# Two-layer network behind bucketed attention: one list-scheduled order for all instructions, a changed row statistic, VectorE low parts, and PV in three parts

## The chip, the cores and the metric

One core of one Trainium2 chip runs the whole program. The metric is the device time of one execution in microseconds (us); lower is better.

## The reference, cut to what matters

`q`, `k`, `v` have the shape (2, 8, 768, 64): 2 batches, 8 heads, 768 rows, 64 columns. Each row of `q` and `k` gets a 6-bit bucket from the signs of its product with `proj`; a row attends only to rows of its own bucket.

```
mask = q_bucket[:, :, :, None] == k_bucket[:, :, None, :]
scores = np.where(mask, scale * (q @ k^T), -1e9)
attn = exp(scores - max); attn = attn / (sum(attn) + 1e-9)
x = (attn @ v) as 1536 tokens x 512
h = x @ w_in                      # layer 0, 512 -> 2048
P = a0 + a1*h + a2*h^2 + a3*h^3;  Q = 1 + |b0|*|h| + |b1|*h^2
x = (P / (Q + 1e-6)) @ w_out      # 2048 -> 512
h = x @ w_in2                     # layer 1
out = (h * clip(h + 3, 0, 6) / 6) @ w_out2
```

## The kernel before, in words

Every fp32 matrix is split into a high part that TensorE takes as it is and a low part (what is left of the value), and a product is made of high x high, high x low and low x high.

**Attention** works on 48 groups (`NG`): a group is 256 query rows of one head, 3 groups to a head, 16 heads in 8 pairs. For a group, `s_mm` makes two score tiles of 128 x 768 on TensorE (two PSUM buffers), `s_max` takes the negated row maximum on VectorE (line 363), `s_exp` makes the exponentials and their row sum on ScalarE into `p`. The row statistics follow: `norm_a` adds 1e-9 and takes the reciprocal on VectorE (lines 375, 376), `norm_v` flags empty rows on GpSimd (line 381), `norm_b` blends the two on VectorE (the helper at line 48, tile `stat`). `norm_p` scales `p` on GpSimd (line 391). `p_mm` transposes `p` on TensorE in three pieces `tt` (line 400), `p_hi` copies each to a high part `pth` on ScalarE (the helper `act`, line 45), `p_lo` subtracts to a low part `ptl` on VectorE (line 413), and `v_mm` multiplies both by `v` in 12 matmuls (line 421). `v_cp` and `v_add` (line 439) join the halves of the result, and `x_hi`, `x_lo` (lines 451, 459) write the two parts of `x`.

For each coming pair of heads, `load_qk` loads q and k, `tp_mm` transposes them (line 227), `tp_hi` writes the high part `th` and a full copy `tf` on ScalarE, `tp_lo` subtracts on GpSimd (line 242), `spread` lays the parts out in `q1`, `q2`, `k1`, `k2` by six DMAs inside SBUF (line 250), `z_mm` and `z_bits` make the bucket bits, and `spread_bits` lays those out (line 272). All DMAs are issued by the SyncE queue (SP).

The order is written out by hand: `slot` goes through the list `SLOT` of 33 operations for s = 0 to 47, each with a lag in groups (scores 0 or one ahead, transposes 2, PV 3, x 4), and each engine takes its instructions in that order.

**Weights** come as 32 units per layer (`order`). A unit is loaded as a 64-bit float block `raw` (line 90), turned into fp32 by `conv_a` and `conv_r` (ScalarE), `conv_s` (VectorE, line 107) and `conv_add` (GpSimd, line 111), and split by `conv_hi` and `conv_lo` (lines 119, 126). The first 11 units (`NPRE`) are converted inside the attention slots; their loads wait, by `pace`, for a score matmul. The next 8 have their place only when the pool `ate` is released, and the last 13 when `atl` is released.

**Layers** run as 96 steps (2 layers x 3 token blocks x 16 column tiles). A step is 12 matmuls into `h` (line 523), a chain on ScalarE and VectorE (helpers at lines 45 and 48), `e_hi` and `e_lo` (line 581), and 12 matmuls into `acc` (line 592). Their order comes from a list scheduler: `plan` gives each operation its engines with durations, a rank and its dependencies, and `ordered` plays them in model time. The last four slots of attention (those for s = 48 to 51) and this list are merged by time with the factor `JOIN`.

## Time and profile before

| | us |
|---|---|
| median of 3 runs | 845.35 |
| lowest, highest | 842.57, 847.24 |
| the profiled execution: device time | 845.65 |
| the profiled execution: span from first to last instruction | 843.9 |
| TensorE busy in the span | 791.7 |
| VectorE busy | 598.9 |
| ScalarE busy | 546.7 |
| GpSimd busy | 405.4 |

The device time of the profiled execution is 1.75 us above its span. Matmuls are pipelined and their ends are modelled, so TensorE's busy time holds overlaps and is not time at its peak; where it matters, starts of consecutive matmuls are compared. Durations of GpSimd are rough. An instruction's own duration can hold time in which it was held up after its start.

### The profile page before, as it was taken

The page shows a single profiled execution, that of the slowest core. Times are in us where ns is not written, and L with a number is a line of the kernel's source. Part 1 is how long each engine was busy: PE and PEld are TensorE (multiplying, and loading weights), DVE is VectorE, ACT ScalarE, POOL GpSimd, SP SyncE. Part 2 cuts the span into 40 slices and gives each one's busy share as a digit, 9 for nine tenths or more (in the row PEclk, how much of TensorE's full clock was granted, in tenths as well). Part 3 has the DMA queues.
Part 4 walks back from the last instruction along what each step waited for, and adds up shares of the span by engine and source line. Part 5 has one row for each costly group of instructions (what it writes and reads, how often), then busy time and mean ns, then how long its engine had stood idle before and what let it go on. Part 6 is the DMA issues. An engine that isn't in the chain of part 4 may idle for free.

```text
span 843.9 us, 12016 instructions
## 1 busy us (share of the span) xinstructions
PE 791.7 (94%) x4042; PEld 665.4 (79%) x4042; DVE 598.9 (71%) x995; ACT 546.7 (65%) x1014; POOL 405.4 (48%) x421
## 2 busy tenths in 40 slices
PE   7998989899888969979999999999999999999997
PEld 5887878888777748757888888888888878887885
DVE  5898989789899788988887798987862232222222
ACT  5988888798889679876768678766671222222221
POOL 5898788788888457762214276657440000000000
PEclk8999999999999979999999999999999999999999
DMA  7754446444552033440002021223420000001001
GB/s 184 188 140 122 115 118 156 105 113 113 135 140 75 11 108 126 146 135 0 1 1 75 1 76 51 75 75 119 154 103 1 13 37 1 1 0 51 1 1 50
DMA packets 46765, 65.72 MB, mean 78 GB/s; under 512 B 28808, under 2 KB 30856, under 8 KB 46704
## 3 DMA queue, kind: packets, MB, share of 16 engines
q1 hardware_dynamic: 46704, 64.96, 27.5%
q8 instruction: 32, 0.52, 0.3%
q14 instruction: 29, 0.24, 0.1%
HBM read 43.00 MB, written 3.15 MB: 55 GB/s over the span
## 4 chain that ended last, share of the span: by engine, by line
PE 64%; DVE 17%; ACT 7%; DMA 6%; issue 4%; POOL 1%; SPq 1%; DVEq 0%; ACTq 0%; POOLq 0%
PE h L523 29%; PE acc L592 27%; PE o L421 4%; DVE ptl L413 4%; DVE stat L363 3%; DVE t L48 3%; DMA q<-th 3%; PE tt L400 2%; DVE stat L375 1%; ACT p L45 1%; DVE bt L266 1%; ACT pth L45 1%; DVE xt L439 1%; DMA nqk<-in_k_dram 1%; ACT tf L45 1%
## 5 line engine op out<-in xcount | busy, mean ns | idle before, releaser
L581 DVE TENSOR_TENSOR gl<-t,gh 128x512 fp32r<-128x512 f32 x48 | 35.0, 728 | 136.7 <-ACT gh L45 114.1
L45 ACT ACTIVATE t<-h,cbias 128x512 f32<-128x512 f32 x48 | 33.0, 688 | 131.5 <-PE h L523 131.5
L111 POOL TENSOR_TENSOR cvd<-cvd,raw 128x512 int32<-128x512 int32 x64 | 89.0, 1396 | 51.3 <-DVE cvd L107 14.5
L581 POOL TENSOR_TENSOR gl<-t,gh 128x512 fp32r<-128x512 f32 x48 | 64.4, 1342 | 101.1 <-ACT gh L45 86.5
L391 POOL TENSOR_SCALAR p<-p,stat 128x768 f32<-128x768 f32 x96 | 93.8, 987 | 35.4 <-DVE stat L48 33.0
L413 DVE TENSOR_TENSOR ptl<-tt,pth 128x512 fp32r<-128x512 f32 x144 | 94.5, 683 | 22.1 <-ACT pth L45 21.3
L45 ACT ACTIVATE p<-s,stat 128x768 f32<-128x768 f32 x96 | 87.2, 908 | 18.2 <-DVE stat L363 17.8
L363 DVE TENSOR_REDUCE stat<-s 128x1 f32<-128x768 f32 x96 | 91.0, 949 | 1.5 <-PE s L356 1.2
L421 PE MATMUL o<-pth,sv 128*128 128x256 f32 x288 | 75.4, 298 | 17.4 <-ACT tf L45 10.1
L400 PE MATMUL tt<-ident,p 128*128 128x128 f32 x576 | 85.8, 278 | 5.7 <-POOL p L391 2.2
L45 ACT ACTIVATE pth<-tt 128x512 fp32r<-128x512 f32 x144 | 81.0, 601 | 13.5 <-PE tt L400 6.3
L45 ACT ACTIVATE gh<-t 128x512 fp32r<-128x512 f32 x96 | 60.1, 626 | 39.7 <-PE acc L592 39.6
L48 DVE SCALAR_TENSOR_TENSOR t<-t,coef,h 128x512 f32<-128x512 f32 x96 | 71.1, 744 | 17.7 <-ACT r L45 9.0
L400 PEld LDWEIGHTS tt<-ident,p 128*128 128x128 f32 x576 | 67.9, 141 | 18.2 <-ACT tf L45 4.9
L421 PEld LDWEIGHTS o<-pth,sv 128*128 128x128 f32 x288 | 54.5, 189 | 24.2 <-DVE xt L439 12.2
L421 PE MATMUL o<-ptl,sv 128*128 128x256 f32 x288 | 71.0, 283 | 0.5 <-DVE ptl L413 0.5
L48 DVE SCALAR_TENSOR_TENSOR t<-t,r 128x512 f32<-128x512 f32 x96 | 65.1, 682 | 8.6 <-ACT r L45 7.6
L592 PE MATMUL acc<-gh,wo_0h 128*128 128x512 f32 x192 | 54.9, 392 | 5.3 <-ACT gh L45 5.3
L353 PE MATMUL s<-k,q 128*128 128x384 f32 x192 | 57.6, 382 | 1.4 <-ACT p L45 1.4
L592 PE MATMUL acc<-wo_0h,gh 128*128 128x512 f32 x192 | 55.1, 393 | 0.4 <-DVE o L605 0.4
L421 PEld LDWEIGHTS o<-ptl,sv 128*128 128x128 f32 x288 | 54.8, 190 | 0.7 <-DVE ptl L413 0.7
L592 PE MATMUL acc<-gl,wo_0h 128*128 128x512 f32 x192 | 55.3, 395 | 0.0
(128 smaller groups left out, 2051.0 us busy)
## 6 DMA issues: line engine op xcount, KB each, us to landing
raw<-in_moe_w_in_dram SPq DMA_DIRECT2D x32, 512.0 KB
raw<-in_moe_w_out_dram SPq DMA_DIRECT2D x32, 512.0 KB
q<-th SPq DMA_DIRECT2D x30, 192.0 KB
k<-th SPq DMA_DIRECT2D x30, 192.0 KB
nqk<-in_q_dram SPq DMA_DIRECT2D x16, 192.0 KB
nqk<-in_k_dram SPq DMA_DIRECT2D x16, 192.0 KB
nv<-in_v_dram SPq DMA_DIRECT2D x16, 192.0 KB
out_dram<-o SPq DMA_DIRECT2D x12, 256.0 KB
```

The lines of the kernel that those rows point to most:

```text
L45: nc.scalar.activation(out=out, in_=in_, func=func, **kw)
L48: nc.vector.scalar_tensor_tensor(out=out, in0=in0, scalar=scalar, in1=in1, op0=op0, op1=op1)
L111: nc.gpsimd.tensor_tensor(out=d.bitcast(I32), in0=d.bitcast(I32), in1=raw[:, :, 0], op=ALU.add)
L353: nc.tensor.matmul(out=ps[:, n, 0:384], lhsT=q1[:, rs], rhs=k1[:, n * 384:(n + 1) * 384], start=True, stop=False)
L363: nc.vector.tensor_reduce(out=stat[g][:, rr, 0:1], in_=sps[(g, rr)][:, :, 0:384], axis=AX.XY, op=ALU.max, negate=True)
L391: nc.gpsimd.tensor_scalar(out=pt, in0=pt, scalar1=st[:, rr, 3:4], scalar2=st[:, rr, 4:5], op0=ALU.mult, op1=ALU.add)
L400: nc.tensor.transpose(ps[:, kt, rr], ptile[(g, rr)][:, c:c + 128], ident)
L413: nc.vector.tensor_tensor(out=pl, in0=live.pop(("p", g, i)), in1=f(ph), op=ALU.subtract)
L421: nc.tensor.matmul(out=o, lhsT=vs[:, kt].rearrange("p a d -> p (a d)"), rhs=pp[:, kt % 2], start=(kt == 0 and n == 0), stop=(kt == R - 1 a ...
L523: nc.tensor.matmul(out=ps, lhsT=w[:, ws], rhs=x[:, cols(m)], start=(n == 0), stop=(n == 3 * KD - 1))
L581: (nc.gpsimd if eng == "POOL" else nc.vector).tensor_tensor(out=e["gl"], in0=e["2"], in1=f(e["gh"]), op=ALU.subtract)
L592: nc.tensor.matmul(out=acc["o"][i], lhsT=lhsT, rhs=rhs, start=(t == 0 and n == 0), stop=(t == NF - 1 and n == 2))
```

## The change

All of attention is described to the list scheduler, pair by pair and group by group, beside the layers, and one order is played for the whole program after the set-up `start`. The hand-written `SLOT`, the merge with `JOIN` and the pacing of weight loads go. Planned durations, lags and the sizes of four buffer rings (PSUM banks `T`, score tiles `S`, `p`, `pt`) are constants. The two operations that make `babs` and the negated `coef` come ahead of `start`.

The row statistics: GpSimd writes two flags instead of one; VectorE adds the row sum, a constant 1e-9 and the first flag by one `tensor_reduce` over three elements, and takes the reciprocal; the blend `norm_b` goes. The low parts of q and k are made from PSUM by VectorE, and the copy `tf` and GpSimd's subtraction go. `v_hi` and `x_hi` are `tensor_scalar` with one input instead of `tensor_tensor` with a tile of zeros. `v_mm` is issued in three parts of 4 matmuls, each behind its own low part. `in_mm` is issued in four parts of 3 matmuls, each with its own dependencies. In the layers, `conv_hi` is planned for ScalarE or GpSimd only.

```diff
+W = {"S": 0.70, "M": 0.87, "E": 1.0, "NV": 0.46, "A": 0.28, "N": 0.965, "P": 0.44, "H": 0.48, "L": 0.60, "V": 0.475, "OC": 0.34,
+     "VA": 0.34, "XH": 0.35, "XL": 0.69, "TP": 0.33, "TH": 0.47, "TL": 0.50, "Z": 1.05, "ZB": 0.59, "VH": 0.50, "VL": 0.97,
+     "ca": 0.555, "cr": 0.56, "sh": 0.335, "add": 1.26, "hi": 0.52, "hi_P": 0.60, "lo": 0.60, "lo_P": 1.26,
+     "abs": 0.58, "sq": 0.49, "lin": 0.57, "lin_D": 0.66, "den": 0.66, "num": 0.66, "ln": 0.615, "ex": 0.52, "nw": 0.60, "rt": 0.66,
+     "g": 0.60, "rl": 0.57, "min": 0.60, "gh": 0.52, "f0": 0.49, "f1": 0.60, "mm": 0.2265, "dma": 0.60}
+W_LAG = {"PE": 0.25, "DVE": 0.13, "ACT": 0.16, "POOL": 0.09, "SP": 2.2, "NONE": 0.0}
+W_SLOT = 4.9
+W_SOON = 5.0
+W_OUT = 0.0
+W_PREP = 0.0
 AHEAD = 4
-W_SLOT, W_TAIL, JOIN = 6.0, 24.0, 2.4
+RINGS = {"T": 4, "S": 2, "p": 6, "pt": 4}
...
-        nc.gpsimd.tensor_tensor(out=s[:, :, hd % 2], in0=nat[("v", hd)], in1=zero, op=ALU.add)
+        nc.gpsimd.tensor_scalar(out=s[:, :, hd % 2], in0=nat[("v", hd)], scalar1=1.0, scalar2=0.0, op0=ALU.mult, op1=ALU.add)
...
-        ps = live["tp"].pop(0)
         if n == 0:
             hl[hd] = tuple(ate.tile([128, S], F32R, name=f"t{x}", tag=f"t{x}{hd % 2}") for x in "hl")
-        full = ate.tile([128, 384], F32, name="tf", tag="tf", bufs=2)
-        act(hl[hd][0][:, n * 384:(n + 1) * 384], ps, scale=qsc)
-        act(full, ps, scale=qsc)
-        live.setdefault("tf", []).append((hd, n, full))
-
-    def tp_lo():
-        for hd, n, full in live.pop("tf", []):
-            th, tl = (t[:, n * 384:(n + 1) * 384] for t in hl[hd])
-            nc.gpsimd.tensor_tensor(out=tl, in0=full, in1=f(th), op=ALU.subtract)
+        act(hl[hd][0][:, n * 384:(n + 1) * 384], live[("tp", hd, n)], scale=qsc)
+
+    def tp_lo(hd, n):
+        th, tl = (t[:, n * 384:(n + 1) * 384] for t in hl[hd])
+        stt(tl, live.pop(("tp", hd, n)), qsc, f(th), ALU.mult, ALU.subtract)
...
+
+    stats = [cpool.tile([128, 2, 7], F32, name=f"stat{i}") for i in range(4)]
+    for t in stats:
+        nc.vector.memset(t[:, :, 2:3], 1e-9)
...
+    def norm_v(g):
+        st = stats[g % 4]
+        for i, x in ((3, 2.0 ** 126), (5, 1.0 / S)):
+            nc.gpsimd.tensor_scalar(out=st[:, :, i], in0=st[:, :, 0], scalar1=BIG / 2, scalar2=x, op0=ALU.is_ge, op1=ALU.mult)
+
     def norm_a(g):
-        nm, sm, ri, av, bv = (stat[g][:, :, i] for i in range(5))
-        nc.vector.tensor_scalar(out=sm, in0=sm, scalar1=1e-9, scalar2=None, op0=ALU.add)
-        nc.vector.reciprocal(out=ri, in_=sm)
-
-    @group
-    def norm_b(g):
-        st = stat[g]
-        stt(st[:, :, 3], st[:, :, 0], BIG / 2, st[:, :, 2], ALU.is_lt, ALU.mult)
-
-    @group
+        st = stats[g % 4]
+        nc.vector.tensor_reduce(out=st[:, :, 6:7], in_=st[:, :, 1:4], axis=AX.X, op=ALU.add)
+        nc.vector.reciprocal(out=st[:, :, 4], in_=st[:, :, 6])
...
-    def v_mm(g):
+    def v_mm(g, i):
         vs = spl[g // 3]
-        o = live[("o", g)] = psum.tile([128, 256], F32, name="o", tag="T", bufs=4)
-        for kt in range(R):
-            for n, pp in enumerate(pts[(g, kt // 2)]):
-                nc.tensor.matmul(out=o, lhsT=vs[:, kt].rearrange("p a d -> p (a d)"), rhs=pp[:, kt % 2],
+        if i == 0:
+            live[("o", g)] = psum.tile([128, 256], F32, name="o", tag="T", bufs=4)
+        for kt in (2 * i, 2 * i + 1):
+            for n, pp in enumerate(pts[(g, i)]):
+                nc.tensor.matmul(out=live[("o", g)], lhsT=vs[:, kt].rearrange("p a d -> p (a d)"), rhs=pp[:, kt % 2],
                                  start=(kt == 0 and n == 0), stop=(kt == R - 1 and n == 1))
+        pts.pop((g, i))
...
+    def plan_attention():
...
+                    old = [("Z", pr - 1, 0), ("Z", pr - 1, 1), ("SPR", hd - 2)]
+                    add(("TP", hd, n), ("PE", W["TP"]), r, [("LQ", hd)] + old, lambda e, hd=hd, n=n: tp_mm(hd, n), takes=("T",),
+                        earliest=3.0 if pr == 1 else 0.0)
+                    add(("TH", hd, n), ("ACT", W["TH"]), r + 0.6, [("TP", hd, n)], lambda e, hd=hd, n=n: tp_hi(hd, n))
+                    add(("TL", hd, n), ("DVE", W["TL"]), r + 1.2, [("TH", hd, n)], lambda e, hd=hd, n=n: tp_lo(hd, n),
+                        frees=(("TP", hd, n),))
...
+            for hd in (2 * pr, 2 * pr + 1):
+                r = (g0 - 4 + 3 * (hd % 2)) * T
+                add(("SPR", hd), ("SP", 6 * W["dma"]), r, [("TL", hd, 0), ("TL", hd, 1), ("S", 3 * (hd - 2) + 2, 1)], lambda e, hd=hd: spread(hd))
+                add(("SB", hd), ("SP", 2 * W["dma"]), r + 0.1, [("ZB", pr, 0), ("ZB", pr, 1), ("SPR", hd)], lambda e, hd=hd: spread_bits(hd))
...
+        def group(g):
+            hd = g // 3
+            b = g * T
+            odd, last = hd % 2, g >= NG - 5
+            for rr in range(2):
+                add(("S", g, rr), ("PE", W["S"]), b - W_SOON + 1.9 * rr, [("SB", hd), ("SPR", hd)], lambda e, rr=rr: s_mm(g, rr), takes=("S",),
+                    earliest=4.0 if hd == 1 else 0.0)
+                add(("M", g, rr), ("DVE", W["M"]), b - W_SOON + 0.9 + 1.9 * rr, [("S", g, rr), ("N", g - 4, 1)], lambda e, rr=rr: s_max(g, rr))
+                add(("E", g, rr), ("ACT", W["E"]), b - W_SOON + 1.9 + 1.9 * rr, [("M", g, rr)], lambda e, rr=rr: s_exp(g, rr), takes=("p",),
+                    frees=(("S", g, rr),))
+            add(("NV", g), ("POOL", W["NV"]), b - W_SOON + 3.8, [("M", g, 0), ("M", g, 1)], lambda e: norm_v(g), pool)
+            add(("A", g), ("DVE", W["A"]), b - W_SOON + 5.0, [("E", g, 0), ("E", g, 1), ("NV", g)], lambda e: norm_a(g))
+            for rr in range(2):
+                add(("N", g, rr), ("POOL", W["N"]), b - W_SOON + 5.4 + rr, [("A", g)], lambda e, rr=rr: norm_p(g, rr), pool)
+            for i in range(3):
...
+            for i in range(3):
+                add(("V", g, i), ("PE", W["V"]), b + 9.3 + 0.5 * i, [("L", g, i), ("VL", hd), ("V", g, i - 1)], lambda e, i=i: v_mm(g, i),
+                    takes=("T",) if i == 0 else (), frees=(("H", g, i),))
...
+        add(("rel", "S"), ("NONE", 0.0), 0.0, [n for n in every if n[0] == "E"], lambda e: release_s())
+        add(("rel", "e"), ("NONE", 0.0), 0.0, [n for n in every if n[0] in ("S", "VL")], lambda e: release_e())
+        add(("rel", "l"), ("NONE", 0.0), 0.0, every, lambda e: release_l())
...
+        ate.release()
+        mps["mp"] = tc.alloc_tile_pool(name="mp", bufs=1, reuse_waits="tile")
+        wpool[1] = tc.alloc_tile_pool(name="wpool1", bufs=1, reuse_waits="tile")
+
+    def release_l():
+        atl.release()
+        wpool[2] = tc.alloc_tile_pool(name="wpool2", bufs=1, side="right", reuse_waits="tile")
+        acc["o"] = [psum.tile([128, TB], F32, name="acc", tag="T", bufs=4) for _ in range(4)]
...
+        convs = [(0, u) for u in order] + [(1, u) for u in order]
+        rel = {0: [], 1: [("rel", "e")], 2: [("rel", "l")]}
+        gone = [("rel", "S"), ("rel", "e")]
...
+            add(("ld", j), ("SP", W["dma"]), rank - 2 * T, [("add", j - RING["raw"])] + early, lambda e: conv_load(*key))
...
+            add(("hi", j), {"ACT": W["hi"], "POOL": W["hi_P"]}, rank, [("add", j)] + used + rel[wplace[u]], lambda e: conv_hi(*key, e),
+                port=("POOL",))
+            add(("lo", j), {"POOL": W["lo_P"], "DVE": W["lo"]}, rank, [("hi", j)], lambda e: conv_lo(*key, e), port=("POOL", "DVE"))
...
-        start()
-        for i in range(4):
-            (v_hi, v_lo)[i % 2](i // 2)
-        s_mm(0, 0)
-        for s in range(NG):
-            slot(s)
         act(babs, coef[:, 4:6], ACTF.Abs)
         nc.vector.tensor_scalar(out=coef[:, 0:4], in0=coef[:, 0:4], scalar1=-1.0, scalar2=None, op0=ALU.mult)
...
+        start()
+        for _, n, e in todo:
+            work[n][3](e)
```

## Rows read from the trace of the kernel before

**Rows 1.** Busy time by stage: us, busy (xinstructions) of each engine, TensorE clock, DMA.

```profile
16.00:279.00 263.00, 237.56 (x1632) 215.87 (x1632) 238.33 (x442) 225.13 (x461) 218.72 (x264) 0.98 0.51 126
279.00:400.00 121.00, 105.26 (x458) 84.37 (x457) 102.69 (x161) 94.87 (x172) 66.35 (x55) 0.94 0.28 92
400.00:640.00 240.00, 240.00 (x1054) 197.43 (x1053) 195.69 (x282) 172.72 (x297) 113.26 (x92) 1.00 0.20 64
```

**Rows 2.** Chain that ended last, merged: start us, us, what.

```profile
76.64 3.74 DMA q<-th
...
279.01 2.77 PE h L523 x12
...
302.97 1.30 POOL cvd L111
304.29 2.90 DMA raw<-in_moe_w_in_dram
...
821.09 16.35 PE acc L592 x70
```

**Rows 3.** Groups of instructions, whole span: busy us, mean ns; idle before, releasers.

```profile
L375 DVE TENSOR_SCALAR stat<-stat 128x2 f32<-128x2 f32 x48 | 24.3, 505 | 2.6 <-ACT p L45 2.1
L48 DVE SCALAR_TENSOR_TENSOR stat<-stat 128x2 f32<-128x2 f32 x48 | 14.6, 304 | 0.7
L242 POOL TENSOR_TENSOR tl<-tf,th 128x384 fp32r<-128x384 f32 x28 | 28.3, 1014 | 2.8 <-ACT tf L45 2.0 <-ACT pth L45 0.7
L45 ACT ACTIVATE tf<-tp,qsc 128x384 f32<-128x384 f32 x28 | 16.1, 574 | 0.0
L48 DVE SCALAR_TENSOR_TENSOR tl<-tp,qsc,th 128x384 fp32r<-128x384 f32 x4 | 2.3, 613 | 1.2 <-ACT th L45 1.2
```

**Rows 4.** Instructions on the tile `stat`: duration ns min/median/max, first and last start.

```profile
L375 DVE TENSOR_SCALAR stat<-stat x48: 161/537/902, 17.5 to 280.0; 128x2 f32<-128x2 f32 x48
L376 DVE RECIPROCAL stat<-stat x48: 167/168/170, 18.1 to 280.2; 128x2 f32<-128x2 f32 x48
```

**Rows 5.** Waits from 16 to 279 us, VectorE then ScalarE: us, times, longest us.

```profile
DVE ptl L413 <- ACT pth L45: 17.8, 10, 3.6
...
ACT th L45 <- DMA q<-th: 8.3, 5, 2.8
ACT pth L45 <- PE tt L400: 4.5, 15, 0.7
```

**Rows 6.** TensorE in order of time, a PV group: start us, us, instruction.

```profile
81.60 0.39 PE L421 MATMUL o<-pth,sv 128*128 128x256 f32 x1 [1.31 <-ACT tf L45]
81.82 0.28 PE L421 MATMUL o<-ptl,sv 128*128 128x256 f32 x1
81.94 0.28 PE L421 MATMUL o<-pth,sv 128*128 128x256 f32 x1
```

**Rows 7.** TensorE in order of time, the first steps of layer 0.

```profile
299.15 0.79 PE L523 MATMUL h<-xh,wi_0h 128*128 128x512 f32 x1 [2.85 <-DVE t L48]
299.75 0.63 PE L523 MATMUL h<-xl,wi_0h 128*128 128x512 f32 x1
300.17 0.63 PE L523 MATMUL h<-xh,wi_0l 128*128 128x512 f32 x1
...
310.83 0.79 PE L523 MATMUL h<-xh,wi_1h 128*128 128x512 f32 x1 [3.67 <-DVE t L48]
```

**Rows 8.** All engines in order of time, the set-up.

```profile
2.85 0.60 SPq L165 DMA_DIRECT2D pj<-in_proj_dram  x1
...
5.42 0.21 ACT L45 ACTIVATE pjh<-pj 128x6 fp32r<-128x6 f32 x1 [3.40 <-DMA pj<-in_proj_dram]
...
5.50 0.43 SPq L172 DMA_DIRECT2D coef<-in_moe_b_dram  x1
...
5.99 1.05 ACT L45 ACTIVATE th<-tp,qsc 128x384 fp32r<-128x384 f32 x2 [0.36 <-PE tp L227]
...
8.12 1.05 ACT L45 ACTIVATE th<-tp,qsc 128x384 fp32r<-128x384 f32 x2 [1.08 <-PE tp L227]
```

More of the change, by code (lines that the diff above doesn't have):

```diff
@@ L259, in z_mm @@
         for i, (w, t) in enumerate(ops):
[L260 to L261 removed]
+            nc.tensor.matmul(out=z, lhsT=w, rhs=t[:, n * 384:(n + 1) * 384], start=(i == 0), stop=(i == len(ops) - 1))
     def z_bits(pr, n):
@@ L638, in add_conv @@
-            used = [("u1" if u[0] == "o" else "i", free[u])] if layer else []
-            add(("hi", j), {"ACT": 0.62, "DVE": 0.96, "POOL": 0.7}, rank, [("add", j)] + used, lambda e: conv_hi(*key, e), port=("DVE", "POOL"), earliest=tail)
-            add(("lo", j), {"POOL": 1.3, "DVE": 0.69}, rank, [("hi", j)], lambda e: conv_lo(*key, e), port=("POOL", "DVE"))
-        for j in range(len(order) - NPRE):
+            used = [("u1" if u[0] == "o" else "i", free[u]) + (() if u[0] == "o" else (KD - 1,))] if layer else []
@@ L725, in ordered, with room @@
         free, port, held, out, now = {}, 0.0, None, [], 0.0
+        ends, took = {}, {r: [] for r in RINGS}
+        def room(n):
+            for r in work[n][6]:
+                if len(took[r]) >= RINGS[r]:
+                    by = freeing[took[r][-RINGS[r]]]
+                    if done.get(by, 1e9) > now + 1e-9:
+                        return False
+            return True
+        done = {}
         while len(out) < len(work):
@@ L756, in ordered @@
                 heapq.heappush(ready, item)
-            times = [v for v in free.values() if v > now + 1e-9] + [port] * (port > now + 1e-9) + [c[0] for c in coming[:1] if c[0] > now + 1e-9]
-            if not times:
+            while times and times[0] <= now + 1e-9:
+                heapq.heappop(times)
+            nxt = [v for v in free.values() if v > now + 1e-9] + [port] * (port > now + 1e-9) + times[:1]
+            nxt += [c[0] for c in coming[:1]]
+            if not nxt:
                 break
-            now = min(times)
@@ L761, in ordered @@
-        assert len(out) == len(work), [n for n in work if left[n]][:9]
-        return out
-    ends = {}
+            now = max(now, min(nxt))
+        assert len(out) == len(work), [n for n in work if n not in done][:9]
+        return out
+    psb, times = [], []
+    plan_attention()
+    plan_layers()
     todo = ordered()
     with tc.manual_schedule():
-        start()
-        for i in range(4):
-            (v_hi, v_lo)[i % 2](i // 2)
-        s_mm(0, 0)
-        for s in range(NG):
-            slot(s)
```

386 lines of the change are left out of this document (164 added, 222 removed).

## The prediction

> **What bounds the kernel now.** I read the busy time by stage first. From 400 us on, TensorE never pauses: 1054 matmuls in 240 us, one each 0.2277 us [rows 1]. Nothing in the change makes these matmuls fewer, so time can only come from before that. In the attention stage, 16 to 279 us, no engine is full, and two are close: VectorE is busy 238.3 of 263 us and TensorE 237.6, so they idle 24.7 and 25.4 us [rows 1]. ScalarE has 225.1 and GpSimd 218.7.
>
> Then the waits. Of VectorE's idle time, 17.8 us in 10 waits are for `pth`, the high part that ScalarE makes [rows 5]. The chain that ended last says why ScalarE was late: it passes through the DMA `q<-th`, once in most pairs (3.74 us in the row, five waits in all) [rows 2, 5]. `tp_hi` of the next pair overwrites the tile that `spread` is still reading; ScalarE stands behind that DMA, the copies behind it are late, and VectorE stops. The hand-written list puts both in the same slot.
>
> Last the join. Layer 0 starts at 279.0 us and TensorE's last run ends at 821.1 + 16.35 = 837.4 us [rows 2]. The 2304 matmuls of the layers at 0.2277 us are 524.6 us. About 7 us of attention's own matmuls still come after 279 us (an estimate: two to three groups' transposes and PV at about 2.7 us a group). 837.4 - 279.0 - 524.6 - 7 = 26.8 us are lost, all in the stage 279 to 400 or at block ends. The places to see: TensorE stops for 2.85 us before 299.15 and 3.67 us before 310.83, and after each stop its matmuls start 0.42 us apart, at the lower of its two clock levels [rows 7]. In the second stop the chain holds a weight's integer add on GpSimd (1.30 us) and then a weight load (2.90 us): the load could not start until a `raw` buffer was free [rows 2].
>
> **The change part by part.** The sum is made against the profiled execution, 845.65 us, which is 0.3 us above the median of 845.35.
>
> *Row statistics.* Gone from VectorE: 48 additions of 0.505 us and 48 blends of 0.304 us, 24.3 + 14.6 = 38.9 us [rows 3]. New: 48 reductions of 128x2x3. The trace has none so small. Below, 0.161 us, the shortest of the additions; above, 0.505 us, their mean [rows 3, 4]. I take 0.168 us, the reciprocal: same tile, same place in the order, and in 48 cases it stays between 167 and 170 ns, while the addition one instruction earlier spreads from 161 to 902 ns [rows 4]. The additions are thus held up by something that the reciprocal doesn't meet. New cost 48 x 0.168 = 8.1 us; net -30.8 us, at the upper bound 24.2 - 38.9 = -14.7 us.
>
> [...]
>
> *Low parts of q and k.* VectorE gains 28 operations `tl<-tp,qsc,th`; the four that the set-up already has take 0.613 us: +17.2 us. ScalarE loses 28 copies (16.1 us) and GpSimd 28 subtractions (28.3 us) [rows 3]; both have room [rows 1], so I count nothing for them. VectorE's work in attention: -30.8 + 17.2 = -13.6 us.
>
> *What is late next.* VectorE then holds 238.3 - 13.6 = 224.7 us, and TensorE with 237.6 us is the fuller engine. So the attention stage can't lose more than TensorE's 25.4 idle us, whatever VectorE gains.
>
> *PV in three parts.* The matmuls are the same, but a part that starts alone pays: after a wait, the second matmul starts 0.22 us after the first, later ones 0.12 us apart [rows 6]. 96 more starts x 0.10 = 9.6 us at most, nothing if the parts run back to back. The part's wait is for `ptl`; queued behind it on TensorE are the next groups' scores and transposes, and on these wait `s_max` and `p_hi`. More of that below.
>
> *The order.* `tp_hi` now depends in the plan on the spread that it used to collide with, and the plan gives a DMA 2.2 us after its issue; so I take that stall (up to 17.8 us of VectorE's idle time) as mostly gone. I put TensorE's idle time in this stage, with the PV starts in it, at 10 us of the 25.4, because two engines above 90% and a chain through four engines leave no schedule without gaps. Attention: 237.6 + 10 = 247.6 against 263 us, **-15.4 us**; bounds -25.4 us, and above zero if the PV waits bite.
>
> *DMAs.* The first 11 weight loads are no longer paced and stand in SP's order among `spread`, `load_qk` and `load_v`. The number of transfers is the same. A load of 2.90 us [rows 2] ahead of a spread delays it by about that; the plan ranks a spread about three slots (15 us) ahead of its scores, which covers it. Without that cover, 11 x 2.9 = 32 us would be the end.
>
> *The join.* Weight units 11 to 13 can now be loaded and taken as far as `cvd` during attention; only `conv_hi` waits for the pool. That removes the load and add that stand in the chain at 303 us. The two stops are 2.85 + 3.67 = 6.5 us, and some 20 matmuls at the lower clock cost 20 x 0.2 = 4 us. I take **-10 us**, between nothing (the remaining 18 units still have to pass through ScalarE and GpSimd beside the first steps) and -26.8 us.
>
> *Set-up.* `babs` and the negated `coef` now stand ahead of the first `th` on ScalarE and VectorE, and wait for the DMA of `coef`. It is issued until 5.93 us; the `pj` DMA, issued until 3.45, was there at 5.42, so `coef` is there at about 7.9 us. `th` started at 5.99, so the first moves by 2.1 us, the second (8.12) by about 1 [rows 8]. I take **+1.5 us** between these.
>
> `v_hi` and `x_hi` only relieve GpSimd, and its 48 further flags lie in its idle time (263 - 218.7 = 44.3 us [rows 1]): nothing. Without that cover they would come between the row sums and VectorE's reduction. Sum: 845.65 - 15.4 - 10 + 1.5 = **822 us**.
>
> **The rivals.**
>
> *Slower: TensorE waits for each PV part.* Where: in attention, on TensorE's queue, 48 x 3 = 144 waits for `ptl`, each behind two engines (`tt` to `pth` to `ptl`). At w us each, attention is 237.6 + 10 + 144w; the whole gain of 23.9 us is gone at w = 0.17 us. At 0.3 us it is 43.2 us, and the time 822 + 43 = 865 us. For it: the chain of three hand-overs is short of slack, and ScalarE already waits for TensorE's transposes 15 times for 4.5 us [rows 5]. Against: the scheduler fills TensorE with other groups' work between part and low part, and two score tiles let it run ahead. [...]
>
> *Only VectorE's work counts.* The order has as many gaps as the old one and the join is as before: 845.65 - 13.6 + 1.5 = 834 us. For it: hand-made and planned order meet the same four nearly full engines.
>
> *Packed.* Attention idles 3 us on TensorE and the join loses only 7: 845.65 - 22.4 - 20 + 1.5 = 805 us. For it: the plan knows the buffer rings and the DMA delay.
>
> *It doesn't do what it says.* The reduction is held up as the addition was, VectorE has -14.7 + 17.2 = +2.5 us, and half of the join's gain remains: 845.65 + 2.5 + 1.5 - 5 = 845 us.
>
> **How the numbers follow.** A measurement of this kernel can tell about 0.5% (4.2 us) from no change. Forecast 0.45, packed 0.16, only VectorE's work 0.16: all three faster, 0.77. Not doing what it says: 0.09, within 0.5%. TensorE waiting: 0.14, slower. The range goes from 799 (a little under the packed case) to 847 us (above the case of no effect); it leaves out the slower rival and the far side of the packed one. The forecast's own range is 812 to 832 us.
>
> **What would show it.** Right: VectorE's reduction over `stat` steady near 0.17 us; its waits for `pth` well under 17.8 us and no `q<-th` under ScalarE's; the first matmul into `h` near 265 us; no stop of several us for a weight load in layer 0's first six steps; the first `th` near 8 us. Wrong: TensorE's waits for `ptl` adding up to tens of us, the first `h` at 279 or later, or the time from the first `h` to the end of the span longer than now (843.9 - 279.0 = 564.9 us); and ScalarE waiting for `raw` loads or `spread`, which would mean that the plan's DMA delay is too short.

## The result, and the profile after

The changed kernel takes 855.78 us (median of 4 runs, 855.33 to 856.37), the kernel before on the same chip 845.53 (842.57 to 847.24): ratio 1.0125, 95% interval [1.0096, 1.0155]. It is slower by 1.25%, and the forecast of 822 us, with its range from 799 to 847 us, had the wrong sign. The profiled execution has a span of 854.6 us.

Busy time by stage, attention first, then three windows counted from the first `h` (269.7 us), columns as in [rows 1]:

```profile
16.00:270.00 254.00, 235.59 (x1667) 221.18 (x1668) 234.05 (x438) 217.36 (x449) 190.85 (x286) 0.99 0.55 137
...
269.70:390.70 121.00, 110.91 (x471) 88.42 (x470) 107.48 (x164) 91.10 (x160) 66.84 (x53) 0.95 0.25 79
390.70:630.70 240.00, 220.04 (x923) 174.25 (x922) 192.92 (x276) 149.97 (x256) 106.89 (x84) 0.98 0.20 62
```

The same two windows of the kernel before, counted from its first `h` at 278.9 us:

```profile
278.90:399.90 121.00, 105.26 (x457) 84.41 (x457) 102.69 (x161) 94.97 (x172) 66.35 (x55) 0.94 0.28 92
399.90:639.90 240.00, 240.00 (x1054) 197.40 (x1053) 195.78 (x282) 172.72 (x297) 113.36 (x92) 1.00 0.20 64
```

Two things happened. Attention became shorter: the first `h` comes 9.2 us earlier (278.9 to 269.7). The layers became longer: from the first `h` to the end, 584.9 us instead of 565.0. The join is not where it went: in the first 121 us TensorE does 14 matmuls more than before. The loss lies in the next 240 us, where [rows 1] had no pause at all: 923 matmuls instead of 1054, and 131 x 0.2277 = 29.8 us. Some of that is won back in the other windows; from the first `h` to the end the loss is 584.9 - 565.0 = 19.9 us.

The parts that the prediction costed, as groups of the whole span (with those of [rows 3], the copies `tf` and GpSimd's `tl` are gone) and on the tile `stat` (duration ns min/median/max, as [rows 4]):

```profile
L53 DVE SCALAR_TENSOR_TENSOR tl<-tp,qsc,th 128x384 fp32r<-128x384 f32 x32 | 19.0, 609 | 6.8 <-ACT th L50 6.7
```

```profile
L336 DVE TENSOR_REDUCE stat<-stat x48: 140/149/163, 20.1 to 268.4; 128x2 f32<-128x6 f32 x48
L337 DVE RECIPROCAL stat<-stat x48: 167/168/171, 20.3 to 268.6; 128x2 f32<-128x2 f32 x48
```

Waits from 16 to 270 us (us in total, times, longest), for [rows 5]:

```profile
PE s L313 <- ACT p L50: 10.5, 11, 1.9
PEld o L368 <- DVE ptl L360: 10.1, 19, 2.2
...
PE o L368 <- DVE ptl L360: 5.3, 10, 1.9
...
DVE ptl L360 <- ACT pth L50: 4.5, 11, 1.3
...
ACT th L50 <- DMA q<-th: 1.4, 1, 1.4
```

VectorE's wait for `pth` fell from 17.8 to 4.5 us, ScalarE's for `q<-th` from 8.3 to 1.4, as forecast. TensorE's idle time in the stage fell less than forecast, from 25.4 to 18.4 us (254.00 - 235.59) and not to 10: its largest wait is now for the exponentials `p`, which must have read a score tile before its buffer is used again, 10.5 us in 11. In the kernel before, from 16 to 279 us:

```profile
PE s L353 <- ACT p L45: 1.4, 4, 0.6
```

And the waits from 380 to 610 us, in layer 0, which [rows 1] had left no room for:

```profile
ACT t L50 <- DVE t L432: 40.2, 24, 2.7
ACT t L50 <- DVE t L53: 24.0, 25, 1.5
...
PE acc L492 <- ACT gh L50: 18.8, 16, 3.6
```

TensorE now waits 18.8 us for `gh`, the high part of the activation. The chain behind it shows in one step of ScalarE, VectorE and TensorE in order of time (start us, us, instruction):

```profile
427.81 0.74 DVE L432 TENSOR_SCALAR t<-h,coef 128x512 f32<-128x512 f32 x1
...
428.59 0.60 ACT L50 ACTIVATE t<-h 128x512 f32<-128x512 f32 x1 [2.22 <-DVE t L432]
...
429.09 0.62 ACT L50 ACTIVATE gh<-t 128x512 fp32r<-128x512 f32 x1
...
429.23 0.75 DVE L53 SCALAR_TENSOR_TENSOR t<-t,coef,h 128x512 f32<-128x512 f32 x1 [0.67 <-ACT t L50]
...
429.76 1.20 PE L492 MATMUL acc<-gh,wo_0h 128*128 128x512 f32 x4 [0.55 <-ACT gh L50]
...
429.89 0.74 DVE L53 SCALAR_TENSOR_TENSOR t<-t,babs,r 128x512 f32<-128x512 f32 x1
...
430.72 0.72 ACT L50 ACTIVATE t<-t,cbias 128x512 f32<-128x512 f32 x1 [1.02 <-DVE t L53]
...
431.48 0.60 ACT L50 ACTIVATE r<-t 128x512 f32<-128x512 f32 x1
...
432.12 0.69 DVE L53 SCALAR_TENSOR_TENSOR t<-t,r 128x512 f32<-128x512 f32 x1 [0.83 <-ACT r L50]
...
432.72 0.75 DVE L53 SCALAR_TENSOR_TENSOR r<-t,coef,r 128x512 f32<-128x512 f32 x1
...
433.50 0.69 DVE L53 SCALAR_TENSOR_TENSOR t<-t,r 128x512 f32<-128x512 f32 x1
...
434.11 0.74 DVE L432 TENSOR_SCALAR t<-h,coef 128x512 f32<-128x512 f32 x1
...
434.89 0.60 ACT L50 ACTIVATE t<-h 128x512 f32<-128x512 f32 x1 [2.23 <-DVE t L432]
```

Read it as a ring. VectorE's `t<-h,coef` (`e_lin`) ends; 0.04 us later ScalarE's square `t<-h` (`e_sq`) starts, after 2.22 us of idling; when that ends, VectorE's next read of `h` starts, after 0.67 us; then denominator, logarithm (1.02 us of waiting), exponential, VectorE again (0.83 us), three of its operations, and only then the next step's `e_lin`. In a round ScalarE stands for 2.22 + 1.02 us and VectorE for 0.67 + 0.83 us until the other engine has ended an operation. A round takes 434.11 - 427.81 = 6.30 us, and TensorE needs 24 x 0.2277 = 5.46 us for a step.

`e_sq` takes nothing from `e_lin`; both only read `h`. That they take turns is no dependency of the plan: for `e_sq` it lists the in-matmuls and an older `e_den`. In the rows above the square starts 0.04 us after the other read of `h` has ended (427.81 + 0.74 and 428.59, 434.11 + 0.74 and 434.89); what makes it wait is not shown. Where the list puts `e_sq` ahead of `e_lin`, it doesn't wait (433.23 in the rows of e10, below).

The same rows show a second thing that the plan doesn't have. Two operations that follow on one engine keep the planned distance where the second doesn't use the result of the first: the denominator starts 0.66 us after VectorE's read of `h` (429.23, 429.89), and 0.66 is planned. Where the second does use it, the distance is longer than planned: the exponential starts 0.76 us after the logarithm (430.72, 431.48; planned 0.615), and `e_g` 0.78 us after `e_rt` (432.72, 433.50; planned 0.66). In the 27 and 28 such pairs from 380 to 560 us that no wait parts, the medians are the same 0.76 and 0.78.

A third thing differs. `e_lin` may stand on ScalarE or VectorE, and the planner chooses by the durations. All of its instructions, the kernel before first (duration ns min/median/max, first and last start):

```profile
L45 ACT ACTIVATE t<-h,coef x33: 665/682/711, 298.0 to 558.4; 128x512 f32<-128x512 f32 x33
L532 DVE TENSOR_SCALAR t<-h,coef x15: 739/750/752, 286.0 to 553.1; 128x512 f32<-128x512 f32 x15
```

```profile
L432 DVE TENSOR_SCALAR t<-h,coef x43: 737/744/753, 274.2 to 579.4; 128x512 f32<-128x512 f32 x43
L50 ACT ACTIVATE t<-h,coef x5: 689/691/693, 282.0 to 501.0; 128x512 f32<-128x512 f32 x5
```

Before, 33 of 48 were on ScalarE, and from 380 to 610 us the square waits for `e_lin` on VectorE once, 0.3 us; now 5 are, and it waits 24 times, 40.2 us.

### The profile page after: what moved, and what is told of

It is laid out like the page before. It is cut to its first block, busy times and chain, and to the rows that moved or that the text cites. A ratio compares the mean times of both kernels' runs of the same rounds, so it can differ in the third digit from the quotient of the medians.

```text
span 854.6 us, 11830 instructions
## 1 busy us (share of the span) xinstructions
PE 796.7 (93%) x4042; PEld 670.7 (78%) x4042; DVE 607.7 (71%) x1005; ACT 522.7 (61%) x962; POOL 377.0 (44%) x439
## 4 chain that ended last, share of the span: by engine, by line
PE 45%; DVE 28%; ACT 12%; DMA 5%; issue 5%; POOL 4%; SPq 1%; ACTq 0%; POOLq 0%; DVEq 0%
PE acc L492 18%; PE h L424 17%; DVE t L53 10%; DVE ptl L360 4%; ACT t L50 4%; PE o L368 4%; DVE stat L320 3%; PE tt L349 3%; DVE t L432 2%; ACT r L50 2%; DVE r L53 2%; DVE cvd L112 2%; PE s L313 2%; DMA raw<-in_moe_w_in_dram 2%; ACT p L50 1%
## 5 line engine op out<-in xcount | busy, mean ns | idle before, releaser
L341 POOL TENSOR_SCALAR p<-p,stat 128x768 f32<-128x768 f32 x96 | 95.9, 1007 | 35.1 <-DVE stat L337 21.1
L53 DVE SCALAR_TENSOR_TENSOR t<-t,h 128x512 f32<-128x512 f32 x48 | 33.0, 687 | 101.3 <-ACT t L50 101.2
L368 PE MATMUL o<-pth,sv 128*128 128x256 f32 x288 | 81.0, 305 | 3.8 <-DVE ptl L360 3.2
L349 PE MATMUL tt<-ident,p 128*128 128x128 f32 x576 | 80.3, 274 | 1.2 <-DVE xt L385 0.7
L492 PE MATMUL acc<-gh,wo_0h 128*128 128x512 f32 x192 | 60.1, 421 | 22.6 <-ACT gh L50 21.4
L368 PE MATMUL o<-ptl,sv 128*128 128x256 f32 x288 | 77.7, 296 | 2.9 <-DVE ptl L360 2.6
L53 DVE SCALAR_TENSOR_TENSOR t<-t,r 128x512 f32<-128x512 f32 x96 | 65.7, 685 | 20.4 <-ACT r L50 18.8
L481 DVE TENSOR_TENSOR gl<-t,gh 128x512 fp32r<-128x512 f32 x47 | 37.2, 791 | 49.6 <-PE acc L492 44.9
L492 PEld LDWEIGHTS acc<-gh,wo_0h 128*128 128x128 f32 x192 | 36.3, 197 | 38.4 <-ACT gh L50 31.8
L313 PE MATMUL s<-k,q 128*128 128x384 f32 x192 | 54.8, 367 | 10.6 <-ACT p L50 10.5
```

What stands on the lines that cost most here:

```text
L53: nc.vector.scalar_tensor_tensor(out=out, in0=in0, scalar=scalar, in1=in1, op0=op0, op1=op1)
L313: nc.tensor.matmul(out=ps[:, n, 0:384], lhsT=q1[:, rs], rhs=k1[:, n * 384:(n + 1) * 384], start=True, stop=False)
L341: nc.gpsimd.tensor_scalar(out=pt, in0=pt, scalar1=st[:, rr, 4:5], scalar2=st[:, rr, 5:6], op0=ALU.mult, op1=ALU.add)
L349: nc.tensor.transpose(ps[:, kt, rr], ptile[(g, rr)][:, c:c + 128], ident)
L368: nc.tensor.matmul(out=live[("o", g)], lhsT=vs[:, kt].rearrange("p a d -> p (a d)"), rhs=pp[:, kt % 2], start=(kt == 0 and n == 0), stop=( ...
L481: (nc.gpsimd if eng == "POOL" else nc.vector).tensor_tensor(out=e["gl"], in0=e["2"], in1=f(e["gh"]), op=ALU.subtract)
```

## The experiments

Each is the changed kernel or the kernel before with the edit shown or described; `...` marks what is cut from an edit. None leaves out work.

**Where the loss is.** The first theory was that the output matmuls of a step are listed too early, three steps behind its in-matmuls. e1 lists them two steps later; e2 forces a distance of three on the kernel before; e3 puts the four in-parts back into one item.

```diff
-            ro = r + 2.5 * T
+            ro = r + 4.5 * T
```

> The changed kernel, with the planned rank of the second matmuls of a step (out_mm) two step lengths later, so that the planned order puts 5 steps' first matmuls ahead of a step's second matmuls in place of 3. Theory (no reserve): TensorE's queue in layer 0 waits for the high part gh because only three steps are in flight; with five the 21 us of these waits go, the time from the first matmul into h to the end of the span falls from 584.7 us to 565 or less, and the time is near 833 us. Rival (the split of in_mm into four parts, or the planned engines of the weight conversion, make the loss): the time stays between 850 and 858 us.

Measured 837.12 us, ratio 0.9872 [0.9835, 0.9909]; first `h` at 269.5, from there to the end 564.3. Later output matmuls take the loss away, though the square still waits 21.1 us for `e_lin` from 380 to 610 us.

```diff
-            add(("i", m), ("PE", W_MM), r, [(x, m - 2) for x in last] + wi + [("i", m - 1)], lambda e, m=m: in_mm(m))
+            add(("i", m), ("PE", W_MM), r, [(x, m - 2) for x in last] + wi + [("i", m - 1), ("o", m - 3)], lambda e, m=m: in_mm(m))
```

> The kernel before, with one more dependency in its plan: a step's first matmuls come behind the second matmuls of the step three earlier, so that 3 steps are in flight in place of 4 to 7. Nothing else is changed. Theory (no reserve): TensorE begins to wait for gh in layer 0, some 20 us are lost and the time is near 865 us. Rival: the lead doesn't matter, the time stays at 845 us within 4 us.

Measured 851.86, ratio 1.0057 [1.0035, 1.0078]. A distance of three costs the old plan some 5 us, not 20.

```diff
...
-                add(("i", m, kk), ("PE", 3 * W["mm"]), r + kk * 3 * W["mm"],
...
+            add(("i", m, KD - 1), ("PE", 12 * W["mm"]), r,
+                [(x, m - 2) for x in last] + [("i", m - 1, KD - 1)] + gone + every_i,
+                lambda e, m=m: [in_mm(m, kk) for kk in range(KD)])
```

> The changed kernel, with in_mm planned as one operation of 12 matmuls as before. The planned lead is 5 steps at the start of layer 0 but 3 from the fifth step on. Theory (no reserve): TensorE still waits for gh in layer 0, the time is 848 to 858 us. Rival (the split makes the loss): near 835 us.

Measured 859.91, ratio 1.0139 [1.0099, 1.0179], with TensorE's waits for `gh` at 21.4 us in the whole span, as in the changed kernel: the split is not the cause.

e5 leaves out the 0.15 us that the kernel before plans between dependent operations of one engine. Its planned distance falls to three, as in the changed kernel.

```diff
-                    ends[x] = max(ends.get(x, 0.0), now + c + W_LAG.get(e, W_SEM))
+                    ends[x] = max(ends.get(x, 0.0), now + c + (0.0 if work[x][0].keys() == {e} else W_LAG.get(e, W_SEM)))
```

> The kernel before, whose list scheduler lets an operation that follows one on its own engine start without the planned 0.15 us between them, as the changed kernel's does. The planned lead of TensorE falls from 4 to 7 steps to 3 or 4; the attention slots are the same. Theory (the gap made the lead): TensorE waits for gh in layer 0 as in the changed kernel, 10 to 20 us are lost, 855 to 865 us. Rival (other durations or the joined order make the loss): 845 us within 4 us.

Measured 837.41, ratio 0.9918 [0.9885, 0.995]: faster, with a distance of three, which neither expectation had. The first theory falls: the distance alone is not it.

**The planned durations.** What was left is the table `W`. The change plans the layers' operations with the spacing of operations that run back to back (den 0.66), the kernel before with their whole duration (0.74). e9 and e10 give the changed kernel the older values, e13 and e14 one half of them each, e15 gives e5 the change's.

```diff
+W.update({'abs': 0.68, 'sq': 0.58, 'lin': 0.69, 'lin_D': 0.74, 'den': 0.74, 'num': 0.74, 'ln': 0.72, 'ex': 0.6, 'nw': 0.69, 'rt': 0.74, 'g': 0.69, 'rl': 0.69, 'min': 0.69, 'gh': 0.62, 'f0': 0.59, 'f1': 0.68})
+W.update({'ca': 0.66, 'cr': 0.67, 'hi': 0.62, 'hi_P': 0.7, 'lo': 0.69, 'lo_P': 1.3, 'sh': 0.42, 'add': 1.3})
```

The first line alone is e13, the second e14, both e10; e9 also has `'mm': 0.21583`.

> The changed kernel, planned with the layer durations of the kernel before (elementwise operations 0.58 to 0.74 us where the change plans 0.49 to 0.66; conversions 0.62 to 1.30; a step of 24 matmuls 5.18 us where the change plans 5.44). The planned lead of in_mm over out_mm stays at three steps, as in the changed kernel; the work is the same, and only the order differs. Theory A (the change's short durations give an order in layer 0 in which ScalarE and VectorE take turns with nothing to spare): the waits of TensorE for the high part (acc <- gh, 21 us) fall below 5, first h to the end of the span about 565 us, total 834 to 840. Rival B (a lead of three steps is what costs, whatever the durations): about 855, with the 21 us of waits still there.

> As the run before this one, but the matmuls keep the change's planned 0.2265 us (5.44 us a step): only the elementwise and conversion durations are the longer ones of the kernel before. Theory A in the form 'the elementwise durations decide': 834 to 840, as with the matmuls changed too. Form 'the planned step shorter than the real one decides' (a plan that has TensorE at 5.18 us always asks for elementwise work sooner than the chip can): about 855 here, and 837 only in the run before. Rival B: 855 in both.

Measured 823.08 (ratio 0.9712 [0.9673, 0.975]) and 822.01 (0.9703 [0.9678, 0.9729]). Theory A, that the short durations make the loss, holds, with more gained than its 834 to 840 us, and the planned matmul is not what decides. Both are faster than either kernel.

> The changed kernel with only the elementwise durations of the layers planned as in the kernel before (abs 0.68 for 0.58, den 0.74 for 0.66, and so on); the weight conversions keep the change's shorter values. With both sets longer it took 822.0. If the elementwise durations alone carry the gain: first h to the end 554 to 560 us, no waits of TensorE for gh worth 5 us, total 820 to 830. If the conversions carry it: about 855, h to the end near 585.

> The complement: only the weight conversions are planned longer (0.555 to 0.66 on ScalarE, 1.26 to 1.30 on GpSimd), the elementwise operations as in the change. If the elementwise durations carry the gain: about 855 with the 20 us of waits for gh still there, the attention part as far as conversions matter there (first h 265 to 270). If the conversions carry it: 820 to 830. If each carries half: about 838 here and in the run before.

Measured 833.61 (0.9866 [0.9842, 0.9889]) and 856.32 (1.0127 [1.0104, 1.0149]). The elementwise durations alone carry 22 of the 34 us. The conversions alone change the total by nothing; they bring the first `h` from 269.7 to 264.9 and, only together with the others, a further 6.5 us in the layers.

The edit of e15, beside that of e5, cut to three of its lines:

```diff
-W_MM, W_LOAD, W_SEM, W_LAG = 2.59, 2.0, 0.15, {"DMA": 2.0, "NONE": 0.0}
+W_MM, W_LOAD, W_SEM, W_LAG = 2.718, 2.0, 0.15, {"DMA": 2.0, "NONE": 0.0}
...
-                el("e_den", ("DVE", 0.74), 4.0, [("e_sq", m), ("e_abs", m), ("e_lo", m - RING["t2"])], e_den)
+                el("e_den", ("DVE", 0.66), 4.0, [("e_sq", m), ("e_abs", m), ("e_lo", m - RING["t2"])], e_den)
...
-                el("e_ln", ("ACT", 0.72), 4.9, [("e_den", m), ("e_ex", m - RING["t4"])], e_ln)
+                el("e_ln", ("ACT", 0.615), 4.9, [("e_den", m), ("e_ex", m - RING["t4"])], e_ln)
...
```

> The reverse, in the other kernel: before without the planned gap on one engine (837.4 in its own run) and, besides, all layer durations of its planner set to the change's shorter ones. If short planned durations make the loss in any list order: TensorE waits for gh or for t by 15 to 25 us in layer 0, total 850 to 860. If they only do so together with something else of the changed order (the operations of attention in the same list, the in-matmuls in four items): 835 to 842.

Measured 874.01, ratio 1.035 [1.032, 1.038]; e5, without the short durations, had 837.41. The loss comes with the short durations in the other kernel too, and larger than expected. Its waits from 380 to 610 us, and behind them the only such wait of the kernel before:

```profile
ACT t L45 <- DVE t L532: 42.8, 25, 2.6
PE acc L592 <- ACT gh L45: 15.8, 19, 2.5
```

```profile
ACT t L45 <- DVE t L532: 0.3, 1, 0.3
```

The kernels side by side (us; from 380 to 610 us ScalarE's waits for `e_lin` and TensorE's for `gh`; last, how many of the 48 `e_lin` stand on ScalarE; e6 and e12 are e1 with one more edit each, shown further down):

| kernel | time | first `h` | `h` to end | `e_lin` (times) | `gh` | on ScalarE |
|---|---|---|---|---|---|---|
| before | 845.5 | 278.9 | 565.0 | 0.3 (1) | 0 | 33 |
| after | 855.8 | 269.7 | 584.9 | 40.2 (24) | 18.8 | 5 |
| e3 | 859.9 | 269.2 | 588.8 | 28.6 (15) | 17.6 | 6 |
| e14 | 856.3 | 264.9 | 587.8 | 35.6 (20) | 16.1 | 4 |
| e15 | 874.0 | 279.9 | 591.0 | 42.8 (25) | 15.8 | 3 |
| e1 | 837.1 | 269.5 | 564.3 | 21.1 (13) | 0 | 8 |
| e6 | 850.9 | 271.0 | 574.1 | 18.9 (10) | 0 | 7 |
| e12 | 870.8 | 290.7 | 578.7 | 19.4 (12) | 0 | 9 |
| e2 | 851.9 | 280.4 | 569.5 | 4.7 (7) | 1.7 | 1 |
| e13 | 833.6 | 269.7 | 561.9 | 5.9 (8) | 0 | 8 |
| e5 | 837.4 | 279.4 | 555.3 | 7.1 (10) | 0 | 19 |
| e10 | 822.0 | 264.9 | 555.4 | 7.7 (10) | 0 | 12 |

The four slowest in the layers (after, e3, e14, e15) are the four in which TensorE waits more than 15 us for `gh`. All four have the short elementwise durations, and the square waits 28.6 us or more in 15 times or more. That the short durations make this loss is shown in both kernels (the changed kernel against e13; e15 against e5, there with the conversions and the matmul). What it is in the order that they make is read from the traces alone: no run changed the turns at `h` by themselves, nor the distances of dependent operations. The engine of `e_lin` alone is not it: e2 has 1 of 48 on ScalarE, with the longer durations, and its layers take 569.5 us. Why e6 and e12 are 9.8 and 14.4 us longer in the layers than e1, without waits for `gh` in this window, stays open.

How e10 gets out of the ring, in order of time, ScalarE and VectorE:

```profile
428.64 0.60 ACT L51 ACTIVATE t<-h 128x512 f32<-128x512 f32 x1 [0.82 <-DVE t L433]
...
432.64 0.66 ACT L51 ACTIVATE r<-h,babs 128x512 f32<-128x512 f32 x1 [0.50 <-PE h L425]
...
433.23 0.59 ACT L51 ACTIVATE t<-h 128x512 f32<-128x512 f32 x1
...
433.56 0.69 DVE L54 SCALAR_TENSOR_TENSOR t<-t,r 128x512 f32<-128x512 f32 x1
...
434.16 0.74 DVE L433 TENSOR_SCALAR t<-h,coef 128x512 f32<-128x512 f32 x1
```

At 428.64 the square still waits for `e_lin`; one step later it is listed ahead of it and doesn't wait, while VectorE is still at the step before. What ScalarE waits for there is `h` from TensorE (0.50 us, ahead of the absolute value `r<-h,babs`), as it should where TensorE is the bound.

e17 is e10 with the edit of e1, and e18 is e10 with longer operations still:

```diff
+W.update({x: 1.12 * W[x] for x in ('abs', 'sq', 'lin', 'lin_D', 'den', 'num', 'ln', 'ex', 'nw', 'rt', 'g', 'gh')})
```

> Both cures in one kernel: the longer planned durations (822.0 alone) and the output matmuls ranked two steps later (837.1 alone). If both remove the same loss, of which the longer durations leave nothing: 819 to 824, and the time from first h to the end within 3 us of 555.4. If they are separate gains that add: 822.0 minus 18 = 804, first h to the end near 537 (2304 matmuls at 0.2277 us are 524.6).

Measured 823.95 (0.9756 [0.972, 0.9792]), `h` to the end 555.5: the two cures remove one and the same loss.

> The longer durations, and the elementwise operations of layer 0 planned another 12 per cent longer (abs 0.76, den 0.83). If slack is what helps, and there is enough of it already: 820 to 825. If the plan can be too loose (it then thinks VectorE the bound of layer 0, and its step 5.7 to 5.9 us instead of 5.44): 826 to 840, with waits of TensorE for gl or gh. If more slack still helps (block 0 of layer 0 takes 104.6 us where a block of 16 steps at 5.46 us takes 87.4): 805 to 818.

Measured 830.29 (0.9834 [0.9803, 0.9864]), `h` to the end 561.8: a plan can be too loose as well. The waits for `gl` or `gh` that were expected with it come to 1.2 us from 380 to 610 us, so where the 6.4 us are lost is not shown.

**The parts in attention.** e4 is the kernel before with the new statistics alone; e8 adds to it the low parts of q and k on VectorE, in the hand-written order.

```diff
-        nc.vector.tensor_scalar(out=sm, in0=sm, scalar1=1e-9, scalar2=None, op0=ALU.add)
-        nc.vector.reciprocal(out=ri, in_=sm)
+        nc.vector.tensor_reduce(out=st[:, :, 6:7], in_=st[:, :, 1:4], axis=AX.X, op=ALU.add)
+        nc.vector.reciprocal(out=st[:, :, 4], in_=st[:, :, 6])
...
```

> The kernel before with the new row statistics alone (one tensor_reduce and a reciprocal on VectorE, two flags on GpSimd, no blend), hand-written order kept. By my term of the prediction 30.8 us of VectorE's work go; if VectorE's work bounds the attention stage, the first matmul into h comes near 255 us and the time is near 822 us. If stalls in the hand-written order bound it (ScalarE behind the spread's DMA), it gains less than half, first h at 267 or later and 834 us or more.

Measured 834.92, ratio 0.9851 [0.9814, 0.9888]; first `h` at 269.3. The statistics alone give what all of the change gives in attention (269.7). The first `h` comes 9.6 us earlier for the 30.8 us that the prediction takes off VectorE's work, so the second case of the expectation holds: that work alone didn't bound the stage.

> The kernel before with the new row statistics and with the low parts of q and k from PSUM on VectorE, hand-written order kept (tp_lo right behind tp_hi). By my terms VectorE gains 17.2 us of work and ScalarE loses 16.1. If VectorE's work bounds the stage, it is slower than with the statistics alone (834.9 us) by up to 17 us; if ScalarE and the waits for pth do, it is faster, by 3 to 10 us.

Measured 863.32, ratio 1.0225 [1.0202, 1.0248]; first `h` at 295.7. VectorE's longest waits from 16 to 290 us:

```profile
DVE tl L48 <- ACT th L45: 30.4, 22, 3.4
DVE tl L48 <- DMA k<-tl: 13.0, 4, 3.6
```

In that order, with the subtraction listed right behind ScalarE's `tp_hi`, VectorE stands at its queue's head for ScalarE's `th`, 30.4 us. e16 undoes the same part in the planned order of e10: a second copy on ScalarE, the subtraction on GpSimd, a ring of two for `tf`.

```diff
...
-        stt(tl, live.pop(("tp", hd, n)), qsc, f(th), ALU.mult, ALU.subtract)
+        nc.gpsimd.tensor_tensor(out=tl, in0=live.pop(("tf", hd, n)), in1=f(th), op=ALU.subtract)
...
```

> The changed kernel with the longer durations (822.0), and the low parts of q and k made as before the change: a second copy on ScalarE (28 more operations) and the subtraction on GpSimd instead of VectorE, both planned. In the hand-written order, putting them on VectorE cost 28 us. If VectorE pays for them in the planned order too: first h 245 to 258 instead of 264.9, total 805 to 816. If the planned order hides them on VectorE, as the prediction had it: first h within 3 us of 264.9, total 820 to 826. If ScalarE or GpSimd is the tighter engine in the planned order: first h 268 to 280, total 826 to 840.

Measured 820.58 (817.12 to 822.46), 0.9704 [0.9673, 0.9735]; with the low parts on VectorE 822.01 (821.61 to 822.55). The totals are the same within 0.2%, so in the planned order the low parts on VectorE cost nothing that is seen. The stages differ: the first `h` is at 269.7 against e10's 264.9, outside the 3 us expected, and from there to the end it takes 548.6 against 555.4. With the low parts on VectorE attention is 4.8 us shorter and the rest 6.8 us longer.

e12 takes e1 and makes PV one item:

```diff
-            for i in range(3):
-                add(("V", g, i), ("PE", W["V"]), b + 9.3 + 0.5 * i, [("L", g, i), ("VL", hd), ("V", g, i - 1)], lambda e, i=i: v_mm(g, i),
...
+            add(("V", g, 2), ("PE", 3 * W["V"]), b + 9.3 + 0.5 * 2, [("L", g, i) for i in range(3)] + [("VL", hd)], lambda e: [v_mm(g, i) for i in range(3)],
...
```

> The changed kernel with later output matmuls (837.1) and, besides, the 12 matmuls of PV as one item of the order, as before the change, instead of three. If the parts save TensorE waits in attention as the prediction had it (between 0 and 9.6 us): first h 271 to 277 instead of 269.5, total 839 to 846. If the parts are worth nothing: 836 to 839, first h within 1 us of 269.5. If each part brings a wait of its own, it gets faster: 830 to 835.

Measured 870.82, ratio 1.0282 [1.0248, 1.0317]: 33.7 us more than e1, 21.2 of them before the first `h` (290.7). The parts are worth more than any of the forecasts. In this edit the four `pt` buffers also come free only with the last part, so what the matmuls' split and the buffers each bring stays open. It is not TensorE's waits for `ptl`: from 16 to 291 us they come to 2.3 us.

Both of the next are e1 with one more edit. e7 moves the set-up operations on `babs` and `coef` behind the first `th`, by an earlier call:

```diff
+        start()
...
-        start()
```

e6 has the first 11 weight loads planned two slots ahead of their conversion at the earliest:

```diff
-            add(("ld", j), ("SP", W["dma"]), rank - 2 * T, [("add", j - RING["raw"])] + early, lambda e: conv_load(*key))
+            add(("ld", j), ("SP", W["dma"]), rank - 2 * T, [("add", j - RING["raw"])] + early, lambda e: conv_load(*key),
+                earliest=max(0.0, (CVS[j] - 2) * W_SLOT) if j < NPRE else 0.0)
```

> The run with the second matmuls planned later, and the two operations on the layer's coefficients behind the set-up, as before the change. My set-up term: the first th comes at 6.0 in place of 8.4 us and the time falls by 1 to 2.1 us, to about 835.5 us. Rival: the loads of v that stand behind three weight loads set the start, and nothing is gained.

> The run with the second matmuls planned later, and the first 11 weight loads not planned before two slots ahead of the slot in which the hand-written order converted them. Theory (the early, unpaced loads and conversions crowd the first 150 us of attention): the first pairs come at about 31 us each in place of 33 to 38, the first matmul into h at 262 us or earlier, the time near 829 us. Rival (the conversions cost the same wherever they stand): first h within 2 us of 269.5, the time 837 us within 3 us.

e7 measured 837.35, ratio 0.9919 [0.9896, 0.9943], e1 837.12: no difference that can be seen, with the first `th` at 6.34 us in place of 8.21. e6 measured 850.87, ratio 1.007 [1.0047, 1.0092]: first `h` 271.0, and the layers 9.8 us longer, which neither expectation had. Pacing the loads in this way doesn't help.

**Both gains on the old kernel.** e11 is e4 with the edit of e5.

> The kernel before with two edits only: the new row statistics (hand-written order kept; alone 834.9) and no planned 0.15 us between dependent operations of one engine in the layers' planner (alone 837.4 against 844.4). If the two are gains of different stretches, attention and layers, they add: first h near 269.5 as with the statistics alone, first h to the end about 557, total 825 to 830. If the layers' gain was the cover of the attention's last operations (the join), they don't: 833 to 836.

Measured 826.81, ratio 0.977 [0.9729, 0.981], and 0.9851 x 0.9918 = 0.977: they add.

## Why the prediction was wrong

*What bounds the kernel now: the step that failed.* It read "TensorE never pauses" in the layers and went on "Nothing in the change makes these matmuls fewer, so time can only come from before that". The layers were taken as fixed. But the change replaces the whole table of planned durations by which their operations are listed, and no term of the sum stands for that. From `h` to the end it was +20 us in place of the join's -10; the elementwise durations alone are worth 32.4 us there, with the conversions planned as in e10 (e14 587.8 against 555.4). "The time from the first `h` to the end" stood among the signs of being wrong, but nothing in the sum could make it longer. The full row in [rows 1] said only that the old order kept TensorE fed.

*The slower rival* put the loss at PV, and it lay in the layers: there the square is held for 2.22 us, and behind it the step's other ScalarE work stands. TensorE's waits for `ptl` in attention are 5.3 us in 10, not 43; that its 865 us lies nearer to the measured 855.8 than the forecast does is luck. The new durations are right for operations that don't need each other's result (0.66 planned and measured) and too short for those that do (0.615 planned, 0.76 measured; 0.66 and 0.78). So the plan lacks two things, these distances and the turns at `h`; the older durations (0.72, 0.74) left room. Which of the two costs how much stays open.

*Row statistics.* Right: 149 ns against 168 taken, 7.2 us in all against 8.1, with a spread of 140 to 163 ns. Before, the 38 additions of 0.28 us or more all end 0.02 to 0.03 us after the GpSimd instruction that was under way when they started; in the changed kernel 16 of the reductions lie inside a GpSimd instruction, and they take 0.14 to 0.16 us. One of each, before and after:

```profile
62.94 0.74 POOL L459 TENSOR_TENSOR xl<-xt,xh 128x256 fp32r<-128x256 f32 x1
...
62.98 0.72 DVE L375 TENSOR_SCALAR stat<-stat 128x2 f32<-128x2 f32 x1
```

```profile
62.12 1.08 POOL L214 TENSOR_TENSOR sv<-nv,sv 128x384 fp32r<-128x384 f32 x1
...
62.82 0.15 DVE L336 TENSOR_REDUCE stat<-stat 128x2 f32<-128x6 f32 x1
```

*Low parts.* The work was right (0.609 us each against 0.613); that VectorE takes it on without waits of its own was right for the total in the planned order (e16) and wrong by 28.4 us in the hand-written one (e8 - e4). VectorE is busy for 234.05 us in the stage, not 224.7: among others the planned order puts four low parts of weights on it (4.4 us), which the sum left out.

*PV in parts.* Sized at a cost of 0 to 9.6 us; e12 puts them at 33.7 us saved, with buffers and layers included.

*The order and the join.* The stall at `q<-th` went as forecast. TensorE's idle time of 10 us in attention was 18.4, most of it the wait for `p`. The first `h` was put near 265 us and came at 269.7; in e10 at 264.9. The term of the join counts matmuls at the lower clock: behind the two stops of [rows 7] the granted clock of the kernel before was 0.50, against 1.00 from 400 to 640 us [rows 1]:

```profile
299.15:302.00 2.85, 2.85 (x7) 2.27 (x8) 2.71 (x5) 2.83 (x6) 1.99 (x3) 0.50 0.50 183
310.83:315.50 4.67, 4.67 (x11) 3.70 (x12) 4.47 (x8) 2.08 (x4) 2.99 (x4) 0.50 0.52 146
```

The join was put at -10 us; in e10 `h` to the end is 565.0 - 555.4 = 9.6 us shorter. So with the older layer durations the change comes to the forecast 822 us (822.0), but the terms are not confirmed by that. In the first 121 us from `h`, TensorE idles 11.1 us in e10 against 15.7 before, and 24 matmuls of attention fewer are left behind the first `h`: part of the 9.6 us is work that moved ahead of it, not a join that was closed. And e5, with the old order of attention and the old join, takes 555.3 us from `h` too. The agreement is in part luck.

*Set-up.* The first `th` is at 8.38 us, as worked out (8.1), against the 5.99 of [rows 8]:

```profile
8.38 1.51 ACT L50 ACTIVATE th<-tp,qsc 128x384 fp32r<-128x384 f32 x3
```

The 1.5 us didn't reach the end: e7 regains nothing.
